# DeltaNet attention and a routed mixture of experts: scores, inverses and state of the attention kept in SBUF and PSUM

## The chip, the core and the metric

The kernel runs on one core of one Trainium2 chip. The metric is the device time of one execution in microseconds (us), the median of three runs. Engines: TensorE (PE; PEld is its weight load), VectorE (DVE), ScalarE (ACT), GpSimd (POOL) and SyncE (SP), which here only issues transfers. An execution's span runs from its first to its last instruction.

## What is computed

Attention: for each of 4 batches and 8 heads a state of 48x48 is carried over 768 positions; then 3072 tokens of 384 values go each to the expert of 8 with the highest router value.

```python
k_n = k / (np.linalg.norm(k, axis=-1, keepdims=True) + 1e-06)
for t in range(S):
    y[:, :, t] = np.einsum('bhd,bhde->bhe', q[:, :, t], state)
    v_old = np.einsum('bhde,bhd->bhe', state, kt)
    state = state + bt[:, :, :, None] * np.einsum('bhd,bhe->bhde', kt, vt - v_old)
...
expert_idx = np.argmax(logits, axis=1)
...
    h = np.maximum(x_sorted[lo:hi] @ w1[e], 0.0)
    y_sorted[lo:hi] = h @ w2[e]
return (gate_w[:, None] * y)
```

## The kernel before

The 768 positions are cut into 24 chunks of 32 (`C`), and four chunks make one of six groups. A chunk's 128 partitions hold 4 batches x 32 positions, so a head's products are blocks of 32x32 on the diagonal of the array, or of 128x32 and 32x128 where the state takes part. Inside a chunk the recurrence is a triangular system; its inverse turns the residual into the chunk's contributions.

Five pieces make the attention. `scores` (L164) multiplies keys with keys and queries of a chunk: ScalarE copies key scores to `gr`, VectorE masks query scores to `qk`, and four transfers write the diagonal blocks of `gr` to DRAM (`gram`). `factors` computes the norms, `fin`, `fout` and the scaled values on VectorE and POOL. `solve` reads a group's 128 blocks back, one block per partition (`u`), inverts all of them at once by 30 elimination steps of two dependent VectorE operations (L255, L259), and writes them to DRAM (`solved`). `fetch_step` reads blocks and values back into the chunk's layout (`ub`, `vt`), eight transfers a chunk. `chain` runs a chunk: keys on state (`ph`, L291), residual `R` on VectorE (L296), queries on state (`pq`, L303), inverse on residual (`pz`, L312), copy `Z` on ScalarE (L317), state products (`pw`, L325) added to `states` by VectorE (L333), and the output into `pq` (L339). `route` takes a batch of up to four chunks: transposes (`pxt`), router products (`pl`, L357), some twenty small VectorE operations, the ranks (`pr`), and one indirect write of token numbers to `lists` for each chunk on POOL's queue (L409); these writes follow one another.

The program is written chunk after chunk, scores and solve seven chunks ahead, and a scheduler puts every engine's instructions in order. Each engine then runs its list strictly in that order. After the attention `lists` is read back (`rows`), the tokens are fetched by indirect transfers, and eight experts follow with weights loaded two ahead (L512 to L559). The first load of the weights of experts 1 and 2 waits until the attention's buffers are free, and `rows` stands behind it on SP.

## Time and profile before

| | us |
|---|---|
| median of three runs (831.4 to 833.11) | 832.48 |
| the profiled execution, its own time | 832.73 |
| its span | 831.0 |
| attention, to the first weight load after it | 477 |
| hand-over | 25 |
| experts | 329 |

The page gives the busy time of each engine over the span: PE 597.4, PEld 404.3, DVE 329.8, ACT 109.2, POOL 158.4, with 6900 matmul records. An fp32 product appears as two records, a transpose as one. [...] Shares over the whole span mix the two halves of the program, so the stretches are read apart. In the timeline, "x64" joins records of one line that follow each other, with the time from the first's start to the last's end.

### The profile page before, as it was taken

How to read it: one execution, taken by the hardware profiler on the slowest of the kernel's cores; microseconds unless marked ns; L12 is line 12 of the kernel's file. 1: busy time of each engine (PE TensorE's matmuls, PEld its weight loads, DVE VectorE, ACT ScalarE, POOL GpSimd, SP SyncE). 2: the span in 40 equal slices, each digit the busy share in tenths (PEclk: the TensorE clock that was granted, in tenths of full speed). 3: DMA queues.
4: the chain of work that ended last, by engine and by line, in shares of the span. 5: the costliest groups of instructions: out<-in, count | busy, mean ns of one | idle time of the engine just before them, and what ended most of it. 6: DMA issues, size and time to landing. Idle time of an engine off the chain costs nothing. (4 is left out here: it accounts for less than half of the span.)

```text
span 831.0 us, 16145 instructions
## 1 busy us (share of the span) xinstructions
PE 597.4 (72%) x6900; PEld 404.3 (49%) x6901; DVE 329.8 (40%) x897; ACT 109.2 (13%) x199; POOL 158.4 (19%) x133
## 2 busy tenths in 40 slices
PE   5432658737763872678729407999999999999992
PEld 3322547535653761567718303555555555555551
DVE  5494794497369539645743201110102111110110
ACT  2210202211120220021101000010101111111100
POOL 5212102122120212201020303030313122131101
PEclk9665857776865785588558556999999999999997
DMA  8653545642735585466040192012323334330000
GB/s 322 172 119 77 148 117 134 170 134 49 185 84 139 134 177 179 131 130 118 15 102 22 39 304 56 9 51 93 113 98 112 120 116 150 110 119 24 21 9 19
DMA packets 112363, 91.84 MB, mean 111 GB/s; under 512 B 85238, under 2 KB 96678, under 8 KB 112288
## 3 DMA queue, kind: packets, MB, share of 16 engines
q1 hardware_dynamic: 106704, 80.37, 34.8%
q0 software_dynamic: 4608, 9.47, 3.8%
q8 instruction: 55, 0.90, 0.5%
q10 hardware_dynamic: 976, 0.94, 0.4%
q14 instruction: 20, 0.16, 0.1%
HBM read 70.96 MB, written 21.36 MB: 111 GB/s over the span
## 5 line engine op out<-in xcount | busy, mean ns | idle before, releaser
L521 PE MATMUL phe<-xTe,w1t 128*128 128x448 f32 x384 | 148.8, 548 | 0.0
L164 PE MATMUL pa<-kq 64*128 64x256 f32 x384 | 77.6, 567 | 67.7 <-DMA kq<-in_kq_t_dram 44.3
L537 PE MATMUL pye<-w2t,hT 128*128 128x384 f32 x384 | 125.2, 486 | 0.0
L521 PEld LDWEIGHTS phe<-xTe,w1t 128*128 128x128 f32 x384 | 73.3, 193 | 70.3 <-issue 68.0
L537 PEld LDWEIGHTS pye<-w2t,hT 128*128 128x128 f32 x384 | 73.0, 190 | 51.7 <-issue 3.0
L164 PEld LDWEIGHTS pa<-kq 64*128 64x128 f32 x384 | 55.6, 285 | 82.1 <-issue 61.5
L325 PE MATMUL pw<-Z,kt 32*128 32x96 f32 x736 | 55.2, 327 | 32.9 <-issue 18.0
L255 DVE TENSOR_TENSOR tmp<-u 128x30 f32<-128x30 f32 (+9 forms) x180 | 75.0, 417 | 4.6
L333 DVE TENSOR_TENSOR states<-states,pw 64x384 f32<-64x384 f32 x92 | 50.7, 551 | 54.6 <-PE pw L325 52.6
L526 DVE TENSOR_SCALAR hT<-phe 128x448 f32<-128x448 f32 x32 | 20.0, 625 | 128.0 <-PE phe L521 128.0
L325 PEld LDWEIGHTS pw<-Z,kt 32*128 32x128 f32 x736 | 49.8, 229 | 42.2 <-issue 29.4
L501 POOL DMA_INDIRECT out_dram<-y,rows x24 | 24.0, 999 | 212.1 <-ACT y L546 178.6
L175 DVE TENSOR_TENSOR qk<-pa,cf 128x256 f32<-128x256 f32 x96 | 37.3, 418 | 65.2 <-ACT gr L173 64.5
L259 DVE TENSOR_TENSOR u<-u,tmp 128x30 f32<-128x30 f32 (+9 forms) x180 | 61.0, 339 | 4.3
L409 POOL DMA_INDIRECT lists<-ids,ri x24 | 24.3, 1012 | 194.7 <-DVE ri L407 88.5
L516 DVE COPY xTe<-px 128x448 f32<-128x448 f32 x24 | 14.1, 613 | 89.7 <-PE px L512 89.7
L291 PE MATMUL ph<-states,kq 128*32 128x96 f32 x736 | 36.6, 329 | 15.3 <-DVE states L333 15.0
L173 ACT ACTIVATE gr<-pa 128x512 f32<-128x512 f32 x48 | 28.3, 596 | 143.9 <-PE pa L164 113.6
L312 PE MATMUL pz<-R,ub 32*32 32x48 f32 x1472 | 27.0, 228 | 26.6 <-DMA ub<-solved 15.5
L512 PE MATMUL px<-ident,xin 128*128 128x128 f32 (+1 forms) x96 | 18.9, 303 | 33.6 <-issue 31.5
L312 PEld LDWEIGHTS pz<-R,ub 32*32 32x32 f32 x1472 | 22.8, 124 | 32.7 <-issue 23.7
L530 ACT ACTIVATE hT<-phe 128x448 f32<-128x448 f32 x32 | 17.4, 544 | 153.8 <-PE phe L521 153.8
(87 smaller groups left out, 536.1 us busy)
## 6 DMA issues: line engine op xcount, KB each, us to landing
kq<-in_kq_t_dram SPq DMA_DIRECT2D x24, 512.0 KB
w1t<-in_moe_w_dram SPq DMA_DIRECT2D x8, 1536.0 KB
w2t<-in_moe_w_dram SPq DMA_DIRECT2D x8, 1536.0 KB
kt<-in_k_tok_dram SPq DMA_DIRECT2D x24, 256.0 KB
kb<-in_k_blk_dram SPq DMA_DIRECT2D x6, 768.0 KB
vb<-in_v_blk_dram SPq DMA_DIRECT2D x6, 768.0 KB
sv<-vb SPq DMA_DIRECT2D x6, 768.0 KB
vt<-sv SPq DMA_DIRECT2D x96, 48.0 KB
```

What stands on the lines that cost most here:

```text
L164: nc.tensor.matmul(pa[:, e, pp, :], lhsT=kq[r, 2 * g + pp, 0, :], rhs=kq[r, 2 * g + pp, :, :].rearrange("p j w -> p (j w)"), start=True, s ...
L173: nc.scalar.activation(out=heads(gr), in_=pa[:, :, :, 0:128], func=AF.Copy, scale=-1.0)
L175: nc.vector.tensor_tensor(out=heads(qk)[:, e], in0=pa[:, e, :, 128:256], in1=blockmask.unsqueeze(1).to_broadcast([128, 2, 128]), op=OP.mult,)
L255: nc.vector.tensor_tensor(out=tv, in0=u[:, 0:j, j].unsqueeze(2).to_broadcast([128, j, w]), in1=u[:, j, j + 1 : C].unsqueeze(1).to_broadcas ...
L259: nc.vector.tensor_tensor(out=u[:, 0:j, j + 1 : C], in0=u[:, 0:j, j + 1 : C], in1=tv, op=OP.add)
L291: nc.tensor.matmul(ph[r, 96 * p : 96 * p + 96], lhsT=kq[:, p, 0, r], rhs=states[:, b, p, :], start=True, stop=True, skip_group_check=True,)
L312: nc.tensor.matmul(pz[r, D * h : D * h + D], lhsT=ub[r, h, r], rhs=Rv[r, D * h : D * h + D], start=True, stop=True, skip_group_check=True,)
L325: nc.tensor.matmul(pw[:, bb, 96 * p : 96 * p + 96], lhsT=kt[r, p, :], rhs=Z[r, 96 * p : 96 * p + 96], start=True, stop=True,)
L333: nc.vector.tensor_tensor(out=sv, in0=sv, in1=pv[r, :, :, D * e : D * e + D], op=OP.add)
L409: nc.gpsimd.indirect_dma_start(out=lists, out_offset=bass.IndirectOffsetOnAxis(ap=ri[:, i : i + 1], axis=0), in_=ids[:, ss[i] : ss[i] + 1] ...
L521: nc.tensor.matmul(ph[:], lhsT=w1t[:, s, f * 128 : f * 128 + 128], rhs=xT[:, s, :], start=(s == 0), stop=(s == NK - 1),)
L537: nc.tensor.matmul(py[:], lhsT=hT[:, f, t * 128 : t * 128 + w], rhs=w2t[:, f, :], start=(f == 0), stop=(f == NF - 1),)
```

## The change

Nothing but the loads of the inputs, the tokens for the experts (`xs`) and the router's lists passes through DRAM in the attention any more. `scores` makes compact blocks: for each head and batch one product of 64 partitions by 32 weight columns with 64 moving columns, keys and queries side by side. `keep_scores` masks both on VectorE, straight out of PSUM. `invert` replaces `factors` and `solve`: VectorE transposes 32x32 blocks to put one block on each partition, reads the norms off the diagonal, inverts the two 16x16 blocks on each diagonal together in 14 elimination steps, and transposes back. `across` makes the remaining 16x16 block with two rounds of 32 products on TensorE, a ScalarE copy between them and a VectorE addition after them. `scale_v` scales a chunk's values by eight small ScalarE operations. `update` sums the state in PSUM (`acc`) in two halves; ScalarE and VectorE each copy a part of each half to `states`.

The order is now written by hand (`manual_schedule`). Pieces of `invert` and `route` are generators that yield an estimated cost; `fill(us)` puts as many of them on VectorE as fit the given sum, at three places of a chunk (1.2, 0.4 and 3.2) and at the start. `chore` does the same with pieces of TensorE's work. Scores run nine chunks ahead (`LEAD`). PSUM tiles have one buffer each; `pa` of `scores` and `po` of `across` share one.

```diff
-    def scratch(name, n):
-        return [nc.dram_tensor(f"{name}{i}", (128, n), FP32, kind="Internal").ap()
-                for i in range(NG)]
-
-    grams, solved, scaled = scratch("gram", C * C), scratch("solved", C * C), scratch("sv", C * D)
...
+    psA = att.enter_context(tc.tile_pool(name="psA", bufs=1, space=PSUM))
+    att.enter_context(tc.manual_schedule())
...
+    states = persist.tile([128, 2, 2 * NP, 2 * D], FP32, name="states")
+    acc = psS.tile([128, 2, 512], FP32, name="acc")
...
+    def fill(us):
+        while us > 0 and behind:
+            cost = next(behind[0], None)
+            if cost is None:
+                behind.popleft()
+            else:
+                us -= cost
+
+    def chore(n=1):
+        while n and chores:
+            chores.popleft()()
+            n -= 1
...
+        pa = psA.tile([128, 2, 512], FP32, name="pa", tag="pa")
+        for p in range(NP):
+            for b in range(B):
                 for e in range(2):
                     r = slice(64 * e, 64 * e + 64)
                     nc.tensor.matmul(
-                        pa[:, e, pp, :],
-                        lhsT=kq[r, 2 * g + pp, 0, :],
-                        rhs=kq[r, 2 * g + pp, :, :].rearrange("p j w -> p (j w)"),
-                        start=True, stop=True,
+                        pa[rows_of(b), e, 64 * p : 64 * p + 64],
+                        lhsT=kq[r, p, 0, rows_of(b)], rhs=kq[r, p, :, rows_of(b)],
+                        start=True, stop=True, skip_group_check=True,
                     )
...
+        return pa
+
+    def keep_scores(c, pa):
...
+        for out, part, mask in (
+            (gts[g][:, H * s : H * s + H, :], view[:, :, :, 0:C], mask_g),
+            (qks[c][:], view[:, :, :, C : 2 * C], mask_q),
+        ):
+            nc.vector.tensor_tensor(
+                out=pairs(out), in0=part,
+                in1=mask.unsqueeze(1).unsqueeze(1).to_broadcast([128, 2, NP, C]), op=OP.mult,
+            )
+        if s == GS - 1:
+            behind.append(invert(g))
...
+        nc.vector.transpose(
+            out=full.rearrange("p i j -> p j i"), in_=gt[:].rearrange("p s j -> p j s")
+        )
...
+        for j in range(W - 2, 0, -1):
+            n = W - 1 - j
+            tmp = block.tile([128, W * W // 2], FP32, name="tmp", bufs=3)
+            tv = tmp[:, 0 : 2 * j * n].rearrange("p (k i w) -> p k i w", k=2, w=n)
             nc.vector.tensor_tensor(
-                out=tv, in0=u[:, 0:j, j].unsqueeze(2).to_broadcast([128, j, w]),
-                in1=u[:, j, j + 1 : C].unsqueeze(1).to_broadcast([128, j, w]), op=OP.mult,
-            )
+                out=tv, in0=ud[:, :, 0:j, j].unsqueeze(3).to_broadcast([128, 2, j, n]),
+                in1=ud[:, :, j, j + 1 : W].unsqueeze(2).to_broadcast([128, 2, j, n]), op=OP.mult,
+            )
...
+                out=ud[:, :, 0:j, j + 1 : W], in0=ud[:, :, 0:j, j + 1 : W], in1=tv, op=OP.add
...
+        ub = block.tile([128, GS * H, C], FP32, name="ub", bufs=3)
+        nc.vector.transpose(
+            out=ub[:].rearrange("p s j -> p j s"), in_=full.rearrange("p i j -> p j i")
+        )
...
+        ubs[g] = ub
+        for s in range(GS):
+            chores.append(partial(across, g, s))
...
+    def across(g, s):
...
+        po = psA.tile([128, 2, 512], FP32, name="po", tag="pa")
+        for h in range(H):
+            sh = H * s + h
+            for b in range(B):
+                nc.tensor.matmul(
+                    po[rows_of(b), 0, W * h : W * h + W], lhsT=gt[rows_of(b), sh, :],
+                    rhs=ub[rows_of(b), sh, W:C], start=True, stop=True, skip_group_check=True,
+                )
+        m1 = work.tile([128, H, W], FP32, name="m1")
+        nc.scalar.activation(
+            out=m1[:].rearrange("p h w -> p (h w)"), in_=po[:, 0, 0 : H * W], func=AF.Copy
+        )
+
...
+            part = ub[:, H * s : H * s + H, W:C]
+            nc.vector.tensor_tensor(
+                out=part, in0=part,
+                in1=po[:, 0, 0 : H * W].rearrange("p (h w) -> p h w", h=H), op=OP.add,
+            )
+
+        chores.appendleft(second)
...
+                    for e in range(2):
+                        r = slice(64 * e, 64 * e + 64)
+                        nc.tensor.matmul(
+                            pc[rows_of(b), e, D * p : D * p + D], lhsT=kq[r, p, 0, rows_of(b)],
+                            rhs=states[r, b % 2, NP * (b // 2) + p, D * e : D * e + D],
+                            start=(p == 0), stop=True, skip_group_check=True,
...
+        chore()
+        fill(1.2)
...
+                    pz[rows_of(b), h % 2, h // 2, :], lhsT=ub[rows_of(b), H * s + h, :],
+                    rhs=R[rows_of(b), h, :],
...
+        pa = scores(c + LEAD)
+        Z = work.tile([128, H, D], FP32, name="Z")
+        nc.scalar.activation(out=pairs(Z[:]), in_=pz, func=AF.Copy)
+        keep_scores(c + LEAD, pa)
+
+        def update(first):
...
+                    e = b // 2 if first else 1 - b // 2
+                    at = D * (NP * (b // 2) + p)
+                    nc.tensor.matmul(
+                        acc[64 * e : 64 * e + D, b % 2, at : at + D],
+                        lhsT=kt[rows_of(b), 2 * p + e, :], rhs=Z[rows_of(b), 2 * p + e, :],
...
+            for e in range(2):
+                slot = e if first else 1 - e
+                r = slice(64 * e, 64 * e + D)
+                out = states[r, :, NP * slot : NP * slot + NP, D * e : D * e + D]
+                src = acc[r, :, 192 * slot : 192 * slot + 192].rearrange("q k (p w) -> q k p w", p=NP)
+                if e == 0:
+                    nc.scalar.activation(out=out, in_=src, func=AF.Copy)
+                else:
+                    nc.vector.tensor_copy(out=out, in_=src)
+
...
+            update(True)
...
+        fill(0.4)
+        if c < NS - 1:
+            update(False)
         return pq
...
+    for c in range(LEAD):
+        keep_scores(c, scores(c))
+        if c >= GS - 1:
+            fill(3.5)
+        load_kq(c + LEAD) if c < 2 else None
+    while len(ubs) < 1:
+        fill(0.1)
+    chore(2)
+    scale_v(0)
...
+        load_kq(c + LEAD + 2)
+        load_tok(c + 3)
+        pq = step(c)
...
         if c == ss[0]:
+            while len(routed) < BATCHES.index(ss):
+                fill(0.2)
+                chore()
...
+        chore(2)
+        logits(xg, c - ss[0], pr)
...
+            chore()
+            behind.appendleft(route(ss, xg, pr))
+        fill(3.2)
```

TensorE in the middle of the attention, before: two chunks, where `ph` and `pc` are keys on state, `pq` queries on state and later the output, `pz` the inverse on the residual, `pa` the scores and `pw` the state products.

```order
L291 MATMUL ph<-states,kq 32x96 x2
L303 MATMUL pq<-states,kq 32x96
L291 MATMUL ph<-states,kq 32x96 x14
L303 MATMUL pq<-states,kq 32x96 x15
L312 MATMUL pz<-R,ub_97 32x48 x32
L339 MATMUL pq<-Z,qk 32x48 x32
L164 MATMUL pa<-kq 128x256 x8
L325 MATMUL pw<-Z,kt 128x96 x16
```

After, one chunk: `acc` is the state in PSUM, `po` the two rounds of `across`, `pr` the router.

```order
L366 MATMUL pc<-states,kq 32x48 x32
L381 MATMUL pq<-states,kq 32x96 x16
L449 MATMUL pr<-wg,xT 128x8 x3
L390 MATMUL pc<-R,ub 32x48 x32
L184 MATMUL pa<-kq 32x64 x32
L406 MATMUL acc<-Z,kt 48x48 x16
L425 MATMUL pq<-Z,qk 32x48 x32
L406 MATMUL acc<-Z,kt 48x48 x16
L316 MATMUL po<-ub,gt 32x16 x32
L330 MATMUL po<-m_3855,fdt_109 32x16 x32
L439 MATMUL pr<-ident,xg 128x128 x3
```

The scores moved between the inverse's product and the state's, the state's products stand in two parts around the output, and two rounds of `across` and the router's transposes stand before the next chunk's keys.

VectorE at the end of a solve before: masks and state additions lie among the steps of `solve`.

```order
L175 TENSOR_TENSOR qk<-pa,cf 128x2x128
L259 TENSOR_TENSOR u<-u,tmp 128x9x22
L255 TENSOR_TENSOR tmp<-u 128x184
L175 TENSOR_TENSOR qk<-pa,cf 128x2x128
L259 TENSOR_TENSOR u<-u,tmp 128x8x23
L175 TENSOR_TENSOR qk<-pa,cf 128x2x128
L255 TENSOR_TENSOR tmp<-u 128x168
L333 TENSOR_TENSOR states<-states,pw 64x8x48
L259 TENSOR_TENSOR u<-u,tmp 128x7x24
L333 TENSOR_TENSOR states<-states,pw 64x8x48
```

After, the chunk behind a group's last mask, with the semaphores waited for (Activation is ScalarE, PE TensorE): residual, masks, two state copies with a transpose between them, the addition of `across`.

```order
L372 TENSOR_TENSOR R<-vs,pc 128x2x4x48 [waits PE_49]
L203 TENSOR_TENSOR gt<-pa,cf 128x2x4x32 [waits PE_49]
L203 TENSOR_TENSOR qk<-pa,cf 128x2x4x32
L419 COPY states<-acc 48x2x4x48 [waits DVE_49,Activation_49]
L222 STREAM_TRANSPOSE ut<-gt 128x32x32 [waits DVE_49]
L419 COPY states<-acc 48x2x4x48 [waits Activation_49]
L335 TENSOR_TENSOR ub<-ub,po 128x8x16 [waits PE_49]
```

The state copies now wait for ScalarE, and a transpose of `invert` stands between them.

SP before, from one chunk's load on: scores out, inputs and scores in, blocks and values in, for half a chunk.

```order
L150 DMA kq<-in_kq_t_dram 128x1024
L183 DMA gram<-gr 32x8x32 x4
L192 DMA kb<-in_k_blk_dram 128x1536
L248 DMA u<-gram 128x1024
L194 DMA vb<-in_v_blk_dram 128x1536
L196 DMA bb<-in_beta_blk_dram 128x32
L276 DMA ub_101<-solved 32x8x32
L277 DMA vt<-sv 32x8x48
L276 DMA ub_101<-solved 32x8x32
L277 DMA vt<-sv 32x8x48
L276 DMA ub_101<-solved 32x8x32
L277 DMA vt<-sv 32x8x48
```

After, the same place: the loads of one chunk, the write of a batch of tokens for the experts, and two loads of the next chunks.

```order
L165 DMA kq<-in_kq_t_dram 128x1024
L170 DMA kt<-in_k_tok_dram 128x384
L172 DMA vt<-in_v_tok_dram 128x384
L511 DMA xs<-xg 128x4x385
L165 DMA kq<-in_kq_t_dram 128x1024
L170 DMA kt<-in_k_tok_dram 128x384
L172 DMA vt<-in_v_tok_dram 128x384
```

All transfers of blocks are gone from the queue; a load of keys and two of tokens are left for each chunk.

## Rows read from the trace of the kernel before

**Rows 1.** Stretches of the span: busy us and (instructions) by engine, granted clock, DMA.

```profile
0.00:477.00 477.00, 284.99 (x5908) 238.31 (x5909) 287.58 (x825) 73.68 (x135) 86.67 (x63) 0.70 0.48 126
477.00:502.00 25.00, 0.18 (x1) 0.21 (x2) 0.00 (x0) 0.00 (x0) 2.83 (x3) 0.50 0.80 263
502.00:831.00 329.00, 312.24 (x992) 165.81 (x991) 42.25 (x72) 35.52 (x64) 68.87 (x68) 0.97 0.24 76
```

**Rows 2.** The page's slices, busy tenths of each fortieth (20.8 us).

```profile
PE   5432658737763872678729407999999999999992
...
DVE  5494794497369539645743201110102111110110
```

**Rows 3.** Waits of the span: who for whom, total us, times, longest.

```profile
PE pa L164 <- DMA kq<-in_kq_t_dram: 44.3, 5, 16.2
...
PE pz L312 <- DMA ub<-solved: 38.1, 3, 22.5
```

**Rows 4.** VectorE by line and shape: out<-in, count, busy us, mean ns, idle before.

```profile
L175 DVE TENSOR_TENSOR qk<-pa,cf 128x256 f32<-128x256 f32 x96 | 37.3, 418 | 65.2 <-ACT gr L173 64.5
...
L296 DVE TENSOR_TENSOR R<-vt,ph 128x384 f32<-128x384 f32 x23 | 12.7, 553 | 13.4 <-PE ph L291 12.6 <-DMA gram<-gr 0.7
...
L249 DVE TENSOR_TENSOR u<-u,fin 128x1024 f32<-128x1024 f32 x6 | 7.3, 1212 | 0.0
...
L255 DVE TENSOR_TENSOR tmp<-u 128x240 f32<-128x240 f32 x12 | 4.9, 407 | 0.3
...
L255 DVE TENSOR_TENSOR tmp<-u 128x30 f32<-128x30 f32 x12 | 2.3, 188 | 0.3
```

**Rows 5.** Timeline, VectorE after the last full batch: start, us, line, tile.

```profile
459.70 0.17 DVE L397 TENSOR_TENSOR rk<-pr,cnt 128x8 f32<-128x8 f32 x1 [0.88 <-PE pr L394]
459.89 0.17 DVE L400 TENSOR_TENSOR cnt<-pr,cnt 128x8 f32<-128x8 f32 x1
```

**Rows 6.** ScalarE by line and shape, columns as in rows 4.

```profile
L317 ACT ACTIVATE Z<-pz 128x384 f32<-128x384 f32 x24 | 11.8, 491 | 159.5 <-PE pz L312 159.5
...
L383 ACT ACTIVATE ex<-dl 128x32 f32<-128x32 f32 x5 | 1.1, 229 | 10.4 <-DVE dl L381 10.4
```

**Rows 7.** Timeline, TensorE at 449 to 455; idle before in brackets.

```profile
449.03 0.90 PE L303 MATMUL pq<-states,kq 128*32 128x96 f32 x30
...
449.93 0.88 PE L312 MATMUL pz<-R,ub 32*32 32x48 f32 x64
...
451.48 1.67 PE L325 MATMUL pw<-Z,kt 32*128 32x96 f32 x32 [0.19 <-ACT Z L317]
...
453.89 0.83 PE L357 MATMUL pl<-wg,xT 128*128 128x8 f32 x6
```

**Rows 8.** Two stretches late in the attention, columns as in rows 1.

```profile
448.00:454.00 6.00, 5.39 (x224) 4.72 (x225) 2.19 (x5) 0.88 (x2) 0.00 (x0) 1.00 0.01 3
459.60:464.00 4.40, 4.21 (x129) 3.75 (x128) 1.90 (x10) 0.12 (x1) 0.97 (x1) 0.50 0.39 138
```

**Rows 9.** Timeline, TensorE at 459 to 464.

```profile
459.59 1.51 PE L291 MATMUL ph<-states,kq 128*32 128x96 f32 x32
...
462.31 1.50 PE L312 MATMUL pz<-R,ub 32*32 32x48 f32 x64
```

**Rows 10.** Timeline, POOL's first list write of the end, SP's first weight load.

```profile
462.78 0.97 POOL L409 DMA_INDIRECT lists<-ids,ri  x1 [27.54 <-DVE ri L407]
...
476.98 0.39 SPq L115 DMA_DIRECT2D w1t<-in_moe_w_dram  x1
```

**Rows 11.** Timeline, the first score products.

```profile
5.21 3.78 PE L164 MATMUL pa<-kq 64*128 64x256 f32 x16 [5.21 <-DMA kq<-in_kq_t_dram]
```

**Rows 12.** First, last and sum of nine stretches with busy TensorE.

```profile
80.00:100.00 20.00, 16.67 (x484) 13.93 (x488) 13.62 (x43) 4.66 (x8) 0.49 (x1) 0.78 0.61 148
...
440.00:460.00 20.00, 16.77 (x509) 14.82 (x503) 7.51 (x23) 3.95 (x9) 0.00 (x0) 0.84 0.07 19
sum 180.00, PE 145.30 PEld 123.47 DVE 83.67 ACT 34.83 POOL 21.35; mean PE 16.14 PEld 13.72 DVE 9.30 ACT 3.87 POOL 2.37
```

## The prediction

> **What bounds the kernel now.** I read the stretches first [rows 1]. The attention runs to 477 us, a hand-over of 25 us follows, and the mixture of experts takes the other 329 us; TensorE is busy 312 of those 329 and nothing of it is touched. So the question is what becomes of the 477 us. There no engine is full: TensorE 285, VectorE 288, ScalarE 74 busy. The slices say why [rows 2]: where VectorE's digit is 9, TensorE's is low, and the other way round. Six groups of four chunks take turns: VectorE solves a group (30 pairs of dependent operations), the result goes out to DRAM and back, then TensorE runs four chunks. The waits name the transfers [rows 3]: 44.3 us of TensorE until keys and queries land, 38.1 us until the solved blocks do. So the bound is a loop of latencies through two engines and the DMA queue. What counts is how long one chunk takes after the change.

> **Prices.** On VectorE [rows 4] 256 elements out of PSUM take 0.42 us, 384 take 0.55, 1024 in SBUF 1.21, 240 take 0.41 and 30 take 0.19; so about 0.157 + 0.00104 per element, and a dependent operation starts some 0.03 after the last one's end (0.17 long, 0.2 apart) [rows 5]. On ScalarE [rows 6] 384 take 0.49, 32 take 0.23. On TensorE every fp32 product is two records. With the clock at 1.00 (448 to 454 [rows 8]), 64 records of 32x32 with 48 columns take 0.88 us (13.8 ns each), 30 of 128x32 with 96 columns 0.90, 32 of 32x128 1.67 and the six router products 0.83 [rows 7]. With it at 0.50 (459.6 to 464 [rows 8]) 64 take 1.50 and 32 of 128x32 1.51 [rows 9]. In 32x128 the weight is four times as wide and a record costs 52 ns, so at these sizes I read the price as that of loading weight columns, and take 13.8 ns for every new record with 32 weight columns, whatever its 16, 48 or 64 moving columns, and 17.5 for the update's 48. No row has a 64x32 tile or a 16-column product. The bounds are below.

> **The change part by part.** Removed: all transfers of gram, solved and scaled blocks, with both waits above, and the large POOL products. Cost of taking them away: none, as nothing waits for POOL's arithmetic afterwards. POOL keeps the 24 list writes, each after the last has landed, some 3.5 us apart [rows 10]; 24 x 3.5 = 84 us lies beside the chunks, but the last four do not (below). SP keeps loads, issued three chunks ahead and more; the xs write in front of them waits for a reciprocal, a stall of some us that the lead covers.

> Solve, per group on VectorE: 28 elimination steps, 2240 elements, 28 x (0.157 + 0.03) + 2240 x 0.00104 = 7.6; two transposes of 1024 and one of 512, which no row shows, taken as the product of 1024 (1.21), together 3.1; two products of 512, 1.4; eighteen small ones, 4.0. Sum 16.1. A transposed block may cost from half to twice that product: -1.5 to +3 a group; five of the six groups lie on the path, so -8 to +15 us in all. [...]

> TensorE per chunk, at full clock: keys on state (A) 0.88, queries on state (B) 0.90, router (C) 0.83, inverse on residual (D) 0.88, scores (E) 0.95, update one (F) 0.56, output (G) 0.88, update two (H) 0.56, the two half products of the inverse (I, J) 0.88 each, router transposes (K) 0.55: 8.75. VectorE per chunk: residual 0.55, masks 0.84, two state copies 1.1, an addition 0.29, a quarter of a solve 4.0, a quarter of a routing 0.9: 7.7. Both fit beside each other only in part, because the program order is fixed by hand.

> The chain of a chunk, from the start r of its residual on VectorE, at full clock: D 0.65 to 1.53, E to 2.48, ScalarE's copy of D until 2.07, F 2.5 to 3.06. Now a wait that the built order shows and the source doesn't: VectorE's state copy waits for ScalarE's, and H waits for VectorE's. So ScalarE 3.1 to 3.6, VectorE 3.65 to 4.2, G meanwhile, H 4.25 to 4.8, again ScalarE to 5.34 and VectorE to 5.95. I until 5.7; ScalarE does xg, then I's copy (6.13); J to 7.06, K to 7.6, A to 8.5. The next residual could start at 8.55. It does so only where VectorE has no solve left to do. In the others it is late:
> - the chunk after a group's last mask: 17 small operations (3.6) follow the addition at 7.4: 11.0;
> - the chunk that ends a batch: the router's second product before A (9.0), seven routing operations (1.4), eight eliminations (2.3): 12.75;
> - the one after it: ranks 1.15, list positions 2.2, then seven eliminations, a product and a transpose (3.6): 12.7.
> Queued behind those operations is the residual, and behind it TensorE's D. Four chunks: 8.55 + 11.0 + 12.75 + 12.7 = 45.0.

> Stretch by stretch, full clock: start 54 to the second chunk's residual (keys land as now at 5.2 [rows 11], four scores and masks to 14, the first solve with five more masks 20, part of the second solve 9, first chunk 11); chunks 1 to 4: 48; 5 to 16: 3 x 45 - 1.5 = 133.5 (no scores at the end); 17 to 22, with no solve left: 48.5; the last chunk and the lists: 18.8, of which 14.2 are four list writes as now (462.78 to 476.98 [rows 10]). Sum 302.8.

> The clock: nine stretches of before in which TensorE is 16.14 of 20 us busy, about what I expect here, run at 0.80 in the mean of their granted clocks; the first, the last and their sum stand in [rows 12]. The low stretch of [rows 8] follows a routing, in which TensorE does little, and the new order has such thin pieces (I, J, ranks, K, and waits for VectorE) in every chunk. At 0.5 TensorE's pieces take 1.7 times as long; by the same chain four chunks then come to 15.2 + 16.7 + 17.9 + 16.2 = 66. At 0.80, with 40% of the time low, they take 1 / (0.6/45 + 0.4/66) = 51.6, that is 14.6% more on some 229 us: +33.4. Attention 336.2; with 354.0 after it and the 1.7 by which the profiled execution (832.73) exceeds its span: **691.9 us**. That execution is 0.25 above the median of 832.48, which changes nothing.

> [...]

> **Rivals.**
> - *The clock stays full.* For it: 448 to 454, with chunks in a row and no solve, is at 1.00 [rows 8]. Against it: the mean of 0.80. Attention 302.8, time 658.5; with the cheap transposes 650.
> - *Each new record costs twice as much*, because the 64x32 tiles or 16-column products overlap less than the 32x32 do, or because the clock stays at 0.50 as in [rows 9]. For it: no row has these shapes, and most of TensorE's work is now such. Against it: the four 128x32 columns do overlap. Then four chunks take 66: +107 on 302.8, time 766. [...]
> - *Slower than before: tiles run one after another.* TensorE then pays each record alone. Attention must exceed 477; with 72 us for products of other shapes and the ends, that needs 34 ns or more for each of some 10,600 new records at full clock. 52 ns, as the 32x128 record costs, gives 550 + 72 + 30, time near 1008. Against it: 13.8 ns for four 32x32 tiles in turn, which cannot be unless they overlap.
> - *The copies do not leave the loop.* If loads of keys lag, TensorE waits for them as now (44.3); but these loads go first in SP's order and no small transfers stand between them. Worth up to +20, inside the range.

> **How the numbers follow.** The forecast, 692, has a chance of 0.62; full clock, 658, 0.19; double price, 766, 0.13; tiles in turn, 0.04; 0.02 for no change by an accident of sums. The range must leave out 2 in 10: 650 takes in full clock and cheap transposes; 750 takes in any two of dear transposes (+15), lagging keys (+20) and a clock of 0.65 (+32), and clocks lower still, short of the double price. A measurement of this kernel tells some 0.2% from no change. Faster 0.94, same 0.01, slower 0.05.

> **What would show it.** TensorE should show some 12,600 matmul records instead of 6,900, VectorE some 230 us busy instead of 330, POOL no arithmetic in the attention. The router's last write should land near 336 us and the hand-over and the experts keep their 25 and 329 us. The residual of three chunks in four should wait for VectorE's own queue, and the second update for VectorE's state copy. Records of 64x32 and 16 columns should take 13 to 24 ns each. The prediction is wrong if a transposed block takes over 2.5 us, if those records take over 30, or if the granted clock over the chunks is under 0.6 or over 0.95.

## The result and the profile after

The changed kernel takes 777.5 us (median of four runs, 774.6 to 781.7); ratio to the kernel before on the same chip 0.936, 95% interval 0.930 to 0.943. The forecast was 692, the range 650 to 750. Faster, as forecast, but by 55 us instead of 140. The profiled execution takes 774.58 us with a span of 772.6.

The stretches of the kernel after: start, 22 chunks from the second chunk's residual to the last one's, last chunk and lists, hand-over, experts. Columns as in [rows 1].

```profile
0.00:59.12 59.12, 25.29 (x1241) 21.09 (x1242) 38.04 (x129) 9.22 (x32) 4.01 (x11) 1.00 0.45 159
59.12:402.49 343.37, 264.26 (x10207) 225.19 (x10202) 136.97 (x440) 96.25 (x308) 19.60 (x20) 0.59 0.23 63
402.49:420.11 17.62, 8.40 (x173) 7.10 (x165) 5.26 (x34) 1.68 (x4) 6.66 (x6) 0.50 0.14 47
420.11:443.60 23.49, 0.00 (x0) 0.00 (x0) 0.00 (x0) 0.00 (x0) 1.92 (x2) 0.50 0.84 273
443.60:772.60 329.00, 311.18 (x992) 165.68 (x992) 42.24 (x72) 35.48 (x64) 69.78 (x69) 0.97 0.24 77
```

Forecast for the five: 54, 263.4 (230 at full clock, 14.6% more at 0.80), 18.8, 25, 329. Four hold within 6 us; the second is 80 us too long and makes nearly the whole miss. A chunk takes 343.37 / 22 = 15.6 us, TensorE is busy 264.26 / 22 = 12.0 of them at a granted clock of 0.59, VectorE 6.2.

The page's slices after show the busy tenths of TensorE and VectorE and the granted clock, each fortieth 19.3 us long:

```profile
PE   3268886777787578778782089999999999999992
...
DVE  3963545155454524611221010101010101010100
...
PEclk9998555555576555555855579999999999999997
```

The two engines no longer take turns as in [rows 2]. TensorE is at 7 to 8 all through, and its clock digit is 5 there. The clock over four-chunk periods shows the same; here the second such period, chunk by chunk:

```profile
129.75:146.43 16.68, 10.15 (x455) 8.50 (x459) 2.69 (x7) 3.77 (x12) 2.91 (x3) 0.55 0.29 56
146.43:164.04 17.61, 14.78 (x522) 12.44 (x522) 7.79 (x24) 5.01 (x17) 0.00 (x0) 0.50 0.19 57
164.04:181.56 17.52, 14.10 (x563) 12.26 (x559) 7.34 (x30) 4.64 (x16) 0.00 (x0) 0.60 0.19 56
181.56:197.50 15.94, 12.50 (x429) 10.69 (x429) 11.19 (x40) 4.38 (x14) 0.98 (x1) 0.54 0.36 112
```

Together 67.8 us; the forecast had 45 at full clock and 66 at half.

What TensorE waits for in those 22 chunks (who for whom, total us, times, longest); "issue" is a gap in which the trace names no releaser:

```profile
PE pr L439 <- DVE rk L525: 9.7, 5, 2.4
PE po L316 <- issue: 8.6, 7, 2.3
PE pc L390 <- DVE R L372: 7.5, 9, 1.3
PE po L330 <- issue: 7.5, 10, 1.4
PE pq L425 <- issue: 7.4, 5, 4.3
...
PE acc L406 <- DVE states L419: 1.3, 3, 0.4
```

The residual, on which the forecast's chain turned, costs 7.5 us in all, the state copy 1.3. The two transfers of [rows 3] are gone. All rows with "issue" sum to 41.8 us. They have a place. One such stretch of TensorE's timeline (start, us, line, records, idle before):

```profile
96.11 0.40 PE L406 MATMUL acc<-Z,kt 32*48 32x48 f32 x5 [0.87 <-issue]
96.44 1.50 PE L425 MATMUL pq<-Z,qk 32*32 32x48 f32 x64
97.87 0.89 PE L406 MATMUL acc<-Z,kt 32*48 32x48 f32 x32
98.69 0.60 PE L330 MATMUL po<-m,fdt 32*32 32x16 f32 x27
99.49 0.71 PE L330 MATMUL po<-m,fdt 32*32 32x16 f32 x36 [0.20 <-issue]
```

From gap to gap 5 + 64 + 32 + 27 = 128 records, which with their weight loads are 256 instructions; the two gaps before these lie 255 and 256 records further back each, by the records in the trace. Of the 43 gaps in the 22 chunks 42 lie so, at multiples of 128 records, give or take one or two that the trace lacks; they are 0.2 to 4.3 us long, and about every second such place has one. The page's queue of instructions (packets, MB, share) has 99 packets after and 55 before:

```profile
q8 instruction: 99, 1.62, 0.9%
```
```profile
q8 instruction: 55, 0.90, 0.5%
```

12,596 records and as many loads are 98 times 256. By this count a gap falls where one packet of program ends. The trace's records of this queue have the packets' times too: 42 of the 43 gaps, 41.2 of the 41.8 us, end 1.2 to 1.6 us after a packet has landed, however long its transfer took (0.88 to 3.40 us). At 135.72 and 141.37 us, behind two of the longest gaps (2.1 and 2.3 us), these packets had taken 1.90 and 3.16 us, against 1.0 for the median one. The next packet starts some 1.1 us after TensorE has resumed, and in the 22 chunks no two packets start less than 3.33 us apart. From 60 to 470 us of before the rows with "issue" sum to 25 us in eight gaps, and only five of them, 8.6 us, end so soon behind a packet.

### The profile page after: what moved, and what is told of

The parts are those of the page before. It is cut to its first block, busy times and chain, and to the rows that moved or that the text cites. A ratio compares the mean times of both kernels' runs of the same rounds, so it can differ in the third digit from the quotient of the medians.

```text
span 772.6 us, 27052 instructions
## 1 busy us (share of the span) xinstructions
PE 609.1 (79%) x12596; PEld 419.1 (54%) x12597; DVE 222.5 (29%) x671; ACT 142.6 (18%) x407; POOL 102.0 (13%) x107
## 5 line engine op out<-in xcount | busy, mean ns | idle before, releaser
L676 PEld LDWEIGHTS pye<-w2t,hT 128*128 128x128 f32 x384 | 73.0, 190 | 51.6 <-issue 3.0
L406 PE MATMUL acc<-Z,kt 32*48 32x48 f32 x1472 | 41.0, 265 | 13.0 <-issue 6.6
L419 DVE COPY states<-acc 48x384 f32<-48x384 f32 x46 | 25.8, 560 | 88.6 <-ACT states L417 88.5
L184 PE MATMUL pa<-kq 64*32 64x64 f32 x1536 | 29.2, 303 | 27.8 <-issue 18.9
L349 ACT ACTIVATE vs<-vt,normt 128x48 f32<-128x48 f32 x192 | 45.5, 322 | 0.0
L406 PEld LDWEIGHTS acc<-Z,kt 32*48 32x48 f32 x1472 | 32.6, 170 | 21.0 <-issue 10.4
L425 PE MATMUL pq<-Z,qk 32*32 32x48 f32 x1536 | 34.4, 260 | 9.0 <-issue 8.2
L390 PE MATMUL pc<-R,ub 32*32 32x48 f32 x1472 | 32.5, 260 | 10.6 <-DVE R L372 7.5
L316 PE MATMUL po<-ub,gt 32*32 32x16 f32 x1536 | 25.8, 206 | 17.2 <-issue 8.8
L330 PE MATMUL po<-m,fdt 32*32 32x16 f32 x1536 | 26.5, 205 | 13.5 <-issue 7.5
L449 PEld LDWEIGHTS pr<-wg,xT 128*128 128x128 f32 x144 | 30.1, 304 | 11.6 <-ACT xT L443 6.9
```

The lines of the kernel that those rows point to most:

```text
L184: nc.tensor.matmul(pa[rows_of(b), e, 64 * p : 64 * p + 64], lhsT=kq[r, p, 0, rows_of(b)], rhs=kq[r, p, :, rows_of(b)], start=True, stop=Tr ...
L316: nc.tensor.matmul(po[rows_of(b), 0, W * h : W * h + W], lhsT=gt[rows_of(b), sh, :], rhs=ub[rows_of(b), sh, W:C], start=True, stop=True, s ...
L330: nc.tensor.matmul(po[rows_of(b), 0, W * h : W * h + W], lhsT=fdt[rows_of(b), sh, :], rhs=m1[rows_of(b), h, :], start=True, stop=True, ski ...
L349: nc.scalar.activation(out=vss[c][:, h, :], in_=vt[:, h, :], func=AF.Copy, scale=norms[g][:, H * s + h : H * s + h + 1],)
L390: nc.tensor.matmul(pz[rows_of(b), h % 2, h // 2, :], lhsT=ub[rows_of(b), H * s + h, :], rhs=R[rows_of(b), h, :], start=(c == 0 and h < 2), ...
L406: nc.tensor.matmul(acc[64 * e : 64 * e + D, b % 2, at : at + D], lhsT=kt[rows_of(b), 2 * p + e, :], rhs=Z[rows_of(b), 2 * p + e, :], start ...
```

## The experiments

Theory C: TensorE's work at the low clock sets the chunk, and the clock is low because the new products use small tiles. Theory F: the gaps are packets of program that arrive late; in the text of e3 they are late because of the loads. Rivals: Q, the clock only follows from TensorE's own queue and waits; V, the forecast's, VectorE's queue holds up the residual. Ratios are to the kernel before on the same chip; 0.01 is 8.3 us. The row shown for each kernel is its 22 chunks, columns as in [rows 1].

**Extra large products (e1, e2).**

```diff
+            nc.tensor.matmul(
+                acc[:, 0, 384:512], lhsT=upper, rhs=ident[:], start=False, stop=True,
...
         fill(1.2)
+        warm(1)
         for h in range(H):
```

> The changed kernel with five extra TensorE products a chunk that nobody reads (128x128 weights, 128 columns), one each in front of the inverse's product, both updates, the second router product and the router's transposes: 115 products more. Theory C (the lost time is TensorE's clock: the chunks of after ran at 0.58 in the mean where 0.80 was forecast, and 32x32 tiles with few columns do not hold it up): the granted clock over the chunks rises to 0.75 or more, the mean of the inverse's records falls from 260 ns to under 220, and the time falls by 25 to 60 us although 1.8 to 3 us of work are added to each chunk. Theory Q (TensorE is held up by its own queue and the waits, and the clock follows from the gaps): the clock stays at 0.58 and the time rises by 25 to 50 us.

> The same with three such products at each of the five places, 345 in all, 5 to 9 us of added work a chunk. Theory C: the clock over the chunks reaches 0.9; the chunk then holds 8.75 us of its own work and 5.4 of extra, some 15 us, so the time is within 20 us of after, with full-clock durations (inverse's records at 170 to 200 ns, output 0.88 us for 64). Theory Q: the clock stays below 0.65 and the time rises by 100 us or more.

Measured: e1 785.0 us, ratio 0.944 (0.938 to 0.951); e2 799.3, 0.958 (0.951 to 0.964).

```profile
58.77:408.59 349.82, 287.30 (x10440) 238.53 (x10436) 137.06 (x439) 96.55 (x311) 19.60 (x20) 0.70 0.21 62
...
L164 PE MATMUL acc<-ident,cf 128*128 128x128 f32 x220 | 66.8, 401 | 15.6 <-DVE states L427 13.5 <-issue 1.9
```
```profile
60.47:427.94 367.47, 306.29 (x10900) 266.46 (x10895) 137.15 (x439) 95.64 (x307) 19.65 (x20) 0.85 0.20 59
...
L164 PE MATMUL acc<-ident,cf 128*128 128x128 f32 x660 | 120.2, 329 | 11.1 <-DVE states L427 9.0 <-issue 1.9
```

The second row of each is the extra product by shape (busy, mean ns, idle before). Without these products, TensorE's own work per chunk is (287.30 - 66.8) / 22 = 10.0 and (306.29 - 120.2) / 22 = 8.5 us, against 12.0 in after, at clocks of 0.70 and 0.85 against 0.59. So the clock follows the products that TensorE is given, and the same work shrinks with it: Q, by which it stays, falls. But C's forecast of a gain fell too. The clock of e1 rose to 0.70, not 0.75; e1 adds 3.0 us a chunk for 2.0 saved, and the extra products, which write into `acc`, also wait for state copies (13.5 us). The clock of e2 reached 0.85, not 0.9, and its time, 18 us above after by the ratios, is within the 20 that C gave. The inverse's records, 250 and 219 ns, stayed longer than C had them in both.

**Loads (e3).** Later chunks use the tiles of earlier ones:

```diff
+            if c >= LEAD + 3:
+                kqs[c] = kept[c % (LEAD + 3)]
+                return
...
+        if 4 <= c < NS:
+            kts[c], vts[c] = kept_tok[c % 4]
```

> The changed kernel without the loads of keys behind the first twelve chunks and of tokens behind the first four; the chunks use the tiles loaded earlier. TensorE of after idles 42 us between 59 and 402 us where the trace names no releaser, in gaps of 0.2 to 1.5 us that come after multiples of 128 records. Theory C: the gaps have little to do with the loads, and the time falls by less than 8 us. Theory F (the gaps are TensorE's instructions being fetched behind the loads in the DMA engines): they shrink from 42 us to under 15, and the time falls by 20 to 35 us.

768.2 us, ratio 0.922 (0.916 to 0.928): some 12 us less than after, between the two forecasts. The gaps in the 22 chunks fall only from 41.8 to 34.5 us, so the loads are at most a small part of their cause. The 22 chunks:

```profile
59.75:393.76 334.01, 263.40 (x10212) 224.84 (x10208) 136.92 (x439) 96.64 (x309) 19.64 (x20) 0.62 0.08 25
```

The packets do not come closer together either: the shortest distance between two is 3.35 us without the loads.

**Eliminations (e4).** The two operations of each step are left out:

```diff
         for j in range(W - 2, 0, -1):
             n = W - 1 - j
...
-                out=ud[:, :, 0:j, j + 1 : W], in0=ud[:, :, 0:j, j + 1 : W], in1=tv, op=OP.add
...
             yield 0.16 + 0.0021 * j * n
```

> The changed kernel without the 28 elimination operations of each inverse, the places of everything else kept: VectorE loses 7.6 us a group. By the chain of the prediction three chunks of four have their residual behind these operations, worth about 2.3 + 3.6 us a group and part of the 3.6 of a third, 25 to 35 us over five groups, and 7 in each of the two first solves. Theory C (TensorE at half clock is what each chunk waits for): the five later groups gain under 10 us together, and the time falls by 10 to 20 us, most of it before the first chunk.

776.0 us, 0.930 (0.925 to 0.935), not to be told from after, and less of a gain than either theory gave. The 22 chunks:

```profile
53.71:403.83 350.12, 270.31 (x10220) 231.36 (x10224) 111.80 (x326) 97.31 (x311) 20.33 (x20) 0.55 0.22 62
```

The start is 5.4 us shorter, the chunks are 6.8 longer at a clock of 0.55. This execution is the slowest of four; by the ratios of all, e4 gains some 5 us, which the start alone makes up. Either way less VectorE work buys nothing in the chunks. V is out, at this clock.

**The inverse back on VectorE (e5), larger tiles for keys on state (e6), both (e7).**

```diff
-        for s in range(GS):
-            chores.append(partial(across, g, s))
...
-        for j in range(W - 2, 0, -1):
+        for j in range(C - 2, 0, -1):
```
```diff
-                            pc[rows_of(b), e, D * p : D * p + D], lhsT=kq[r, p, 0, rows_of(b)],
-                            rhs=states[r, b % 2, NP * (b // 2) + p, D * e : D * e + D],
+                        pc[rows_of(b), 0, 96 * p : 96 * p + 96], lhsT=kq[:, p, 0, rows_of(b)],
+                        rhs=states[:, b % 2, NP * (b // 2) + p, :],
```

> The changed kernel with the whole 32x32 inverse on VectorE again (60 elimination operations a group instead of 28, no products between 16x16 blocks), masks and transposes in SBUF kept; VectorE gets 2.4, 1.6, 0.4 and 4.0 us of other work at four places of a chunk. TensorE loses 128 of some 530 records a chunk, by the rows of after 24.4 + 22.4 us over 22 chunks, 2.1 us each, and a quarter of the 42 us of gaps without a releaser; VectorE gains about 14 us a group, 3.5 a chunk, on 6.2. Theory C+F (after is paced by TensorE's records at the lower clock and by the gaps that come with their number): the chunk falls from 15.6 to 12.5 to 13.5 us, the first solve grows by 14, and the time comes to 715 to 745. Theory V (the forecast's: the residual waits behind VectorE's queue in three chunks of four): VectorE's share grows and the time is 780 to 810.

> The changed kernel with one thing as before: keys on state as 16 products of 128x32 with 96 columns for two heads together instead of 32 of 64x32 with 48. 64 of some 1060 records and weight loads a chunk go, but by the rows the piece takes 1.51 instead of 1.03 us at half clock, and 0.90 instead of 0.88 at full. Theory C with the tile's size counting (larger tiles raise the granted clock): clock over the chunks 0.62 or more and the time 0 to 15 us lower. If neither clock nor gaps move, the time rises by 0.5 us a chunk, 11 us.

> Both at once: whole inverse on VectorE, keys on state in 128x32 tiles; some 370 records a chunk instead of 530. Theory C+F: 700 to 735, below e5 if larger tiles raise the clock and by up to 10 us above it if they do not. Theory V: 780 or more.

e5 730.9 us, ratio 0.873 (0.869 to 0.877); e6 770.0, 0.918 (0.913 to 0.922); e7 725.6, 0.866 (0.862 to 0.870). The 22 chunks of each, in this order:

```profile
62.62:356.57 293.95, 223.98 (x7432) 187.45 (x7435) 201.34 (x588) 90.21 (x284) 19.93 (x20) 0.58 0.25 73
```
```profile
59.50:401.62 342.12, 255.68 (x9512) 219.69 (x9508) 137.25 (x439) 96.72 (x309) 19.65 (x20) 0.64 0.23 63
```
```profile
61.85:352.76 290.91, 212.49 (x6722) 181.05 (x6726) 201.13 (x588) 90.22 (x284) 20.28 (x20) 0.64 0.27 73
```

In e5 VectorE is busy 64 us longer in the chunks and the chunk falls from 15.6 to 13.4 us, because TensorE has 27% fewer records; the gaps fall from 41.8 to 13.0. That is C+F's number, and V's opposite. In e6 one piece in larger tiles lifts the clock to 0.64, although the piece is dearer at half clock (1.51 us against 1.03). Over the whole span its four executions show 0.802 to 0.810, against 0.766 to 0.780 for after and, on e6's own chip, 0.781 to 0.795 for e10. By the ratios the time falls 15 us. The 22 chunks, 342.12 us, are only 1.3 us shorter than after's, as the gaps grow to 48.2, but 9.5 shorter than e10's on the same chip. The gaps do not set the clock: e5 has 13.0 us of them at 0.58, e6 48.2 at 0.64. In e7 the larger tiles lift it again, from 0.58 to 0.64; its time lies 6 us below e5's by the ratios, whose intervals just touch.

**Without the two rounds (e12).** 

> The changed kernel without the two rounds of 32 products of 16 columns, ScalarE's copy between them and VectorE's addition; nothing takes their place, so the inverse lacks its 16x16 block off the diagonal. By the rows of after the two rounds hold TensorE 2.1 us a chunk, 46.8 in 22, with 23.9 us of idle time in front of them. Theory C+F: 45 to 75 us less, 703 to 733. If the chunk is set elsewhere, by VectorE's queue or the loads, under 25 us.

```diff
-        for s in range(GS):
-            chores.append(partial(across, g, s))
```

710.3 us, 0.847 (0.840 to 0.854): 74 us less than after by the ratios, at the upper end of C+F's range. The 22 chunks:

```profile
53.78:332.14 278.36, 216.51 (x7432) 182.15 (x7435) 132.58 (x416) 90.19 (x284) 19.87 (x20) 0.62 0.28 77
```

The chunk falls to 12.65 us in this execution, the fastest of five. So the 128 records of `across` cost 3.0 us a chunk where the forecast had 2 x 0.88, and the start 5.3. Of the 3.0 us, 2.2 are busy time and 0.9 gaps, which fall from 41.8 to 23.0 us in the 22 chunks. Of the 74 us e5's longer inverse takes 22 back.

**Order (e10 on after; e8, e11 on e7; e9 with extra products).**

```diff
-        pa = scores(c + LEAD)
+        chore()
         Z = work.tile([128, H, D], FP32, name="Z")
...
             update(False)
+        keep_scores(c + LEAD, scores(c + LEAD))
```

> The changed kernel (777.5 us) with TensorE's order alone altered: a chore (the router's second product, as a rule) behind the inverse's product in the place of the scores, the scores behind the second update. VectorE's other work 2.0, 0.8 and 2.0. In after the waits that this could fill are small (transposes 11.7 us, the first update 5.0 for ScalarE's copy, 22 chunks). Theory C+F: the records and their clock set the chunk, so the order by itself gives 0 to 15 us. If the order alone gave 25 us or more, the hand-made order was a cause of its own in after.

> The kernel with the whole inverse on VectorE and keys on state in 128x32 tiles (725.6 us), with two pieces of TensorE's order exchanged: the router's second product goes behind the inverse's product, where TensorE waits for ScalarE's copy, and the scores go behind the second update, where the transposes wait for ScalarE's copy of the output (20.2 us over 20 chunks). VectorE's other work is spread as 4.4, 1.8, 0.4 and 1.8. Theory C+F (TensorE sets the chunk): the wait of the transposes falls from 1.0 to under 0.3 us a chunk, some 20 us in all, and the time comes to 700 to 712. Theory V (VectorE, 8.9 of 12.1 us busy a chunk, is by now the bound): the wait moves in front of the inverse's product and the time stays within 8 us of 725.

> The same with one extra unread 128x128 product in front of the inverse's product and one in front of the transposes, 46 in all, some 0.6 us each at half clock. If the granted clock rises by 0.06 or more over the chunks, as it did by 0.11 with five of them, the time is 3 to 12 us below the kernel without them; if the pieces of TensorE are no longer what waits, or the clock does not rise, 10 to 25 us above it.

> The kernel with whole inverse, 128x32 tiles and the new order (695.2 us) with VectorE's other work as 3.2, 2.4, 0.6 and 2.0 instead of 4.4, 1.8, 0.4 and 1.8: there the second update waits 19.7 us for VectorE's state copy, which stands behind the first of these sums in the chunks at full clock. If VectorE's place in the queue is what is left, 683 to 692; if TensorE's records are, 693 to 700.

e10 785.3 us, 0.935 (0.927 to 0.944): the order alone gives nothing. e8 695.2, 0.835 (0.829 to 0.841): 26 us by the ratios on e7, more than forecast, with the chunk at 11.9 us. e9 707.8, 0.851 (0.845 to 0.857): the clock rises from 0.69 to 0.76, for which the first branch of its text had a gain; yet by the ratios the time rises by 13 us, as its second branch had it: the extra products alone wait 21.8 us for the state copies. e11 691.8, 0.823 (0.814 to 0.833): the intervals of e8 and e11 overlap, so no gain is shown. The 22 chunks of e10, e8, e9 and e11:

```profile
60.74:412.35 351.61, 263.20 (x10220) 223.34 (x10224) 138.71 (x440) 96.90 (x311) 19.81 (x20) 0.60 0.23 62
```
```profile
60.95:322.04 261.09, 194.94 (x6728) 167.11 (x6732) 201.30 (x588) 90.32 (x284) 20.01 (x20) 0.69 0.30 82
```
```profile
61.02:336.07 275.05, 205.30 (x6848) 175.00 (x6840) 201.21 (x588) 90.95 (x288) 19.88 (x20) 0.76 0.28 77
```
```profile
61.84:320.07 258.23, 196.16 (x6728) 168.31 (x6732) 200.89 (x587) 90.33 (x284) 19.81 (x20) 0.71 0.29 82
...
PE pc L336 <- DVE R L319: 21.2, 15, 2.7
```

The order is worth something only once the records are fewer. Then the waits come that the forecast expected of after itself: 21.8 us of the second update for VectorE's state copy in e8, 21.2 for the residual in e11. e11 is the fastest kernel of the study: by its ratio 147 us below before, 94 below after.

## Why the prediction was wrong

**The clock, the step that failed.** The forecast took 0.80 for the chunks from [rows 12], because TensorE would be about as busy. It is: 12.0 of 15.6 us is 77%, against 81% there. The clock is 0.59. What differs is the work inside the busy time: beside the 32x32 products of both kernels, tiles of 128x32, 32x128 and 64x128 with 96 and 256 columns before, and mostly 32x32 and 64x32 with 16 to 64 columns after. With larger tiles it rose to 0.70 in e1, 0.85 in e2 and 0.64 in e6; which of their measures counts (rows, columns, or fewer records) no run separates. The busy share by itself did not foretell it: 77% goes with 0.59, and in e6 75% with 0.64. By the forecast's own formula 0.59 gives 1 / (0.18/45 + 0.82/66) = 60.9 for four chunks, 311 for the 22: 47 of the 80 us. That alone would have given 739 us, inside the stated range. This split is worked out, not measured.

**The gaps, a term that was missing.** Every price was read from rows without a gap. The forecast put the supply of the program at nothing. Against the remaining 33 us stand 41.8 us of gaps; the 37 us that TensorE further idles in the 22 chunks are waits for other engines, and the forecast's chain held waits of its own. e5 and e12, with 27% fewer records, have 13.0 and 23.0 us of gaps, less than in proportion; e6, with 7% fewer, has 48.2. That a gap ends behind a packet of program is shown by the packets' times (42 of 43, 1.2 to 1.6 us after it landed); no run changed their supply alone. Some 464 records a chunk are 3.6 packets, and at 3.33 us each, the shortest distance seen in after, that makes an estimate of 12.1 us for a chunk; whether packets come closer at a higher clock was not measured. The forecast's chunk was 12.0 at a clock of 0.80 and 10.5 at full clock; if the estimate holds there too, the full clock alone would not have given 658.

**TensorE's prices were right.** At high clock a stretch of e8 shows the inverse, the router, the update and the output at the forecast's 0.88, 0.83, 0.56 and 0.88:

```profile
237.70 0.88 PE L336 MATMUL pc<-R,ub 32*32 32x48 f32 x64 [0.30 <-DVE R L319]
238.52 0.84 PE L396 MATMUL pr<-wg,xT 128*128 128x8 f32 x6
239.28 0.57 PE L351 MATMUL acc<-Z,kt 32*48 32x48 f32 x32
239.78 0.88 PE L370 MATMUL pq<-Z,qk 32*32 32x48 f32 x64
```

At half clock after has 1.50 for the inverse and, for the new shapes, 1.19 for the scores and 1.05 to 1.43 for a round of 16 columns: 16 to 22 ns a record for these, inside the stated 13 to 24. These are prices of single pieces; over many pieces, by the shortest distance of the packets, 128 records take at least 3.33 us, an estimate of 26 ns each. Two small slips in the forecast's sums change nothing: 48, 133.5 and 48.5 make 230, not 229, and the tiles in turn need 35 ns, not 34.

**VectorE's chain did not bind.** At 15.6 us a chunk TensorE leaves VectorE time for the queue that the forecast added up; the three late chunks of four are not there, and TensorE waits 7.5 us in all for the residual. e4 takes work out of this queue, and the chunks gain nothing. The second update waits 1.3 us in all for the state copy.

**Transposes** were dearer than assumed but within the bounds. VectorE by line and shape, after:

```profile
L222 DVE STREAM_TRANSPOSE ut<-gt 128x1024 f32<-128x1024 f32 x6 | 12.4, 2064 | 0.1
...
L300 DVE STREAM_TRANSPOSE fdt<-ut 128x512 f32<-128x512 f32 x6 | 6.3, 1046 | 0.0
```

2.06 us for 1024 instead of 1.21 makes 2 us more a group. Only the start, 59.1 us instead of 54, can hold it, beside products there that already take their half-clock times.

**The rivals.** The one with 0.13 came nearest: its second branch, the clock at 0.50 as in [rows 9], gave 766, 11.5 below the median. That is luck in part: it took 0.50 throughout and no gaps, where the clock was 0.59 and gaps made up the rest. The text named a clock under 0.6 as what would make the forecast wrong, and still gave that case a small chance.

## What to carry over

## What was not expected of the hardware

Gaps of 0.2 to 4.3 us after multiples of 128 records, 43 of them over 80 packets in the chunks, each but one ending 1.2 to 1.6 us behind a packet of program. A transpose of 32x32 blocks at 2.0 ns an element (2.06 us for 1024). And the granted clock reads 1.00 in the first stretch of after, while the inverse's 64 records take 1.48 us there, about the 1.50 that they take at 76.17 us, where it reads 0.50:

```profile
45.65 1.48 PE L390 MATMUL pc<-vs,ub 32*32 32x48 f32 x64
```
```profile
76.17 1.50 PE L390 MATMUL pc<-R,ub 32*32 32x48 f32 x64
```

At the start of this trace the duration of a known product, 1.48 us, is the safer reading.
